# Moving the first weight conversions, the centroid copies and the first value loads in a fused attention and MoE kernel

## The chip, the core and the metric

One core of one Trainium2 chip runs the whole kernel in one launch. The metric is the device time of one execution in microseconds (us). The median of three runs before the change was 805.57 us (804.07 to 806.16).

## What is computed

Three stages follow one another. The first is clustered attention over 2 batches, 8 heads, 768 tokens and head dimension 64: each query and key gets the nearest of 16 centroids of its head, and a query sees only the keys of its own cluster. The other two are gated products on 1536 tokens.

```python
q_assign = argmax(q_n @ c_n.T); k_assign = argmax(k_n @ c_n.T)
scores = where(q_assign == k_assign, q @ k.T / sqrt(D), -1e9)
attn = softmax(scores) @ v            # 16 heads, 768 x 768 each
x = attn as [1536, 512]
x = ((x @ w1) * (x @ w2)) @ w3 @ w_out            # d_ff 1024
out = (sigmoid(x @ w_gate) * (x @ w_val)) @ w_out2   # d_ff 1536
```

## The kernel before

**Precision by splitting.** A float32 operand is split into a high part (`hi`, rounded for the fast matmul) and a rest (`lo`), and products are summed from two or three matmuls. `split` (line 51) makes both parts on the engines that it is given. `move` (line 61) is a DMA on SyncE's queue (SP) from SBUF to SBUF.

**Weights.** They arrive as 64-bit words. `f64_split` (line 84) loads a half of a weight pair (512 KB, line 98, on SP), takes an absolute value on ScalarE (ACT, line 102), limits it (line 108), works on the bits with four VectorE (DVE) steps (lines 110 to 113), adds (line 114), casts to `hi` on ACT (line 115) and subtracts for `lo` on GpSimd (POOL, line 116). `load_pair` (line 118) does this for two halves. For the first two pairs the add of line 114 is on POOL too. The loaded words have three buffers (tag `f64`), so at most three halves can lie in SBUF unconverted. In the traces a half's words are called `w_f`, its work tile `w_a`, its result `w`.

**Start.** TensorE (PE) is kept busy with dummy transposes (`warm`, line 130: 12, then 8, then 50). The centroids are loaded, normalized and transposed, split into `chi` and `clo`, and placed by eight small DVE copies (line 174) into the block matrix `cw`. `load_qk(0)` and `load_v(0)` (lines 188 to 201) issue the first loads: 384 KB each of q, k and v. `prep_split` makes `hi` and `lo` of q and k, and its DVE instructions are held behind the last copy into `cw` (line 395). `prep_scatter` (line 228) moves them by six DMAs per head into the operands `QH`, `KH`, `QX`, `KX`. `prep_sims` (line 243) multiplies them with `cw`. `prep_argmax`, `prep_onehot` and `prep_mask` turn the similarities into one-hot rows that become rows 64 to 95 of `QH` and `KH`. `prep_v` splits v on POOL.

**Attention.** The work goes over 8 head pairs (0 to 7), each 2 heads and 3 blocks of 256 queries, so 48 blocks. `scores(j)` (line 302) is one of 96 tiles of 128 queries: four matmuls (lines 315 to 318), a row maximum on DVE (line 319, `nm`), an exponential on ACT (line 321, `e`). `transposes` (line 324) turns three groups of a block with PE; ACT (line 56) and DVE (line 59) split them into `ph`, `pl` (one group of some blocks on POOL). `weighted_v` (line 343) multiplies with v. Beside this, pair n prepares pair n+1 (split, scatter, similarities, one-hot, mask, v). Pair 6 loads and splits no later pair's q and k, and pair 7 prepares none.

**Where the first weights stand.** At the end of block 36 (first of pair 6) and of block 42 (first of pair 7) the loop traces `load_pair` for weight pairs 0 and 1 (line 445). `tc.issue_after(ins)` puts the instructions traced in its block behind `ins` in the issue order of `ins`'s own engine, and does nothing on other engines. Here `ins` is a DVE instruction, the last mask of head pair 0 (line 285).

**Order of work.** A planner sets each engine's order at build time: an engine takes, of the instructions that it believes ready, the one that stands first in the program; an instruction that stands later is taken earlier if nothing before it is ready. On the chip each engine then runs its list in that order.

**After attention.** From line 510 on the gated products run as long series of matmuls; the first unit needs weight pair 0, the second needs weight pair 1.

Of the kernel before, what the change touches and what calls it, by code (L numbers as in the profile page):

```python
# [11 lines left out]
AF = mybir.ActivationFunctionType  # L12
ALU = mybir.AluOpType
AX = mybir.AxisListType

B, H, S, D, C = 2, 8, 768, 64, 16
NP = H // 2
KT = S // 128
BIG = 2.0 ** 60
# [8 lines left out]
def tile_cluster_attention__then__moe__then__gated_moe(  # L28
# [15 lines left out]
    nc = tc.nc  # L44
# [6 lines left out]
    def split(x, hi, lo, hi_engine, lo_engine):  # L51

        if hi_engine is nc.gpsimd:
            nc.gpsimd.tensor_scalar(out=hi, in0=x, scalar1=1.0, scalar2=1.0, op0=ALU.mult, op1=ALU.mult)  # L54
        elif hi_engine is nc.scalar:
            nc.scalar.copy(hi, x)  # L56
        else:
            nc.vector.tensor_copy(hi, x)
        lo_engine.tensor_tensor(out=lo, in0=x, in1=hi, op=ALU.subtract)  # L59
# [70 lines left out]
    def warm(n, name):  # L130

        pt = ps_t.tile([128, 2, 256], F32, tag="t", name=name)
        for i in range(n):
            nc.tensor.transpose(pt[:, 0, 0:128], ident, ident)
# [28 lines left out]
    cps = ps_a.tile([128, 128], F32, tag="a", name="cps")  # L163
    nc.tensor.transpose(cps, c2.rearrange("p j d -> p (j d)"), ident)
    warm(8, "warm1")
    chi = ctmp.tile([128, 128], F32R, name="chi")
    clo = ctmp.tile([128, 128], F32R, name="clo")
    split(cps, chi, clo, nc.vector, nc.vector)
    for e in range(2):
        rows = slice(64 * e, 64 * e + 64)  # L170
        for w in range(2):
            base = 64 * w + 32 * e
            for g, src in ((0, chi), (1, clo)):
                cw_done = nc.vector.tensor_copy(
                    cw[rows, :, w, base + 16 * g : base + 16 * g + 16],
                    src[rows].bitcast(F32).rearrange("p (n e c) -> p n e c", n=NP, e=2)[:, :, e, :],
                )
# [16 lines left out]
    def load_v(pr):  # L194
        t = core.tile([128, 2, KT, D], F32, tag="vraw", name=f"vraw{pr}", bufs=1)
        nc.sync.dma_start(t, v[pr])
        raw[pr, "v"] = t


    load_qk(0)  # L200
    load_v(0)


    opnd = {}

    def lead(pr):

        return nc.vector if pr == 0 else nc.gpsimd
# [19 lines left out]
    def prep_scatter(pr, e):  # L228
        qh, ql, kh, kl = opnd[pr, "hl"]
        r = slice(64 * e, 64 * e + 64)  # L230
        QH = core.tile([96, S], F32R, tag="QH", name=f"QH{pr}_{e}", bufs=3)
        KH = core.tile([96, S], F32R, tag="KH", name=f"KH{pr}_{e}", bufs=3)
        QX = core.tile([128, S], F32R, tag="QX", name=f"QX{pr}_{e}", bufs=3)
        KX = core.tile([128, S], F32R, tag="KX", name=f"KX{pr}_{e}", bufs=3)
        move(QH[0:64], qh[r])
        move(KH[0:64], kh[r])
        move(QX[0:64], qh[r])
        move(QX[64:128], ql[r])
        move(KX[0:64], kl[r])
        move(KX[64:128], kh[r])  # L240
        opnd[pr, e] = (QH, KH, QX, KX)
# [17 lines left out]
    def prep_argmax(pr):  # L259
        sm = opnd.pop((pr, "sm"))  # L260
        mx = core.tile([128, S // 32], F32, tag="mx", name=f"mx{pr}", bufs=2)
        shape = [128, S // 32, C]
        nc.vector.tensor_reduce(out=mx, in_=sm, axis=AX.X, op=ALU.max)
        nc.vector.tensor_tensor(out=sm, in0=sm, in1=mx.unsqueeze(2).broadcast_to(shape), op=ALU.is_ge)
        lead(pr).tensor_tensor(out=sm, in0=sm, in1=dec.unsqueeze(1).broadcast_to(shape), op=ALU.mult)
        opnd[pr, "code"] = sm
# [13 lines left out]
    def prep_mask(pr, e):  # L280
        ohT = opnd[pr, "oh"]
        QH, KH, _, _ = opnd[pr, e]
        if pr == 0:
            nc.scalar.copy(QH[64:96], ohT[32 * e : 32 * e + 32])
            opnd["masked"] = nc.vector.tensor_scalar(out=KH[64:96], in0=ohT[64 + 32 * e : 96 + 32 * e], scalar1=-1.0, scalar2=BIG, op0=ALU.add, op1=ALU.mult)
            return
        move(QH[64:96], ohT[32 * e : 32 * e + 32])
        move(KH[64:96], ohT[64 + 32 * e : 96 + 32 * e])
# [8 lines left out]

    blocks = [(pr, e, q0) for pr in range(NPR) for e in range(2) for q0 in range(0, S, 256)]
    NB = len(blocks)
    exps, pts, avs, acc_x = {}, {}, {}, {}  # L300

    def scores(j):

        if not 0 <= j < 2 * NB:
            return
        pr, e, q0 = blocks[j // 2]
        QH, KH, QX, KX = opnd[pr, e]
        at = e * KT + q0 // 128 + j % 2
        if at == 0:
            acc_x[pr, "sum"] = core.tile([128, 2 * KT], F32, tag="ss", name=f"ss{pr}", bufs=2)  # L310
        ss = acc_x[pr, "sum"]
        nm = core.tile([128, 1], F32, tag="nm", name=f"nm{j}", bufs=4)
        q = slice(q0 + 128 * (j % 2), q0 + 128 * (j % 2) + 128)
        sp = ps_s.tile([128, 1024], F32, tag="s", name=f"s{j}")
        nc.tensor.matmul(sp[:, 0:512], QH[:, q], KH[:, 0:512], start=True, stop=False)
        nc.tensor.matmul(sp[:, 512:S], QH[:, q], KH[:, 512:S], start=True, stop=False)
        nc.tensor.matmul(sp[:, 0:512], QX[:, q], KX[:, 0:512], start=False, stop=True)
        nc.tensor.matmul(sp[:, 512:S], QX[:, q], KX[:, 512:S], start=False, stop=True)  # L318
        nc.vector.tensor_reduce(out=nm, in_=sp[:, 0:S], axis=AX.X, op=ALU.max, negate=True)  # L319
        et = core.tile([128, S], F32, tag="e", name=f"e{j}", bufs=5)  # L320
        nc.scalar.activation(et, sp[:, 0:S], AF.Exp, bias=nm, accum_out=ss[:, at : at + 1])  # L321
        exps[j] = et

    def transposes(i, k2):
# [19 lines left out]
    def weighted_v(i, k2):  # L344
        if not 0 <= i < NB:
            return
        pr, e, q0 = blocks[i]
        ph, pl = pts.pop((i, k2))
        if k2 == 0:
            avs[i] = ps_a.tile([128, 256], F32, tag="a", name=f"av{i}")  # L350
        av = avs[i]
        for kk in range(2):
            kt = 2 * k2 + kk
            w = opnd[pr, e, "v"][:, kt].rearrange("p j d -> p (j d)")
            nc.tensor.matmul(av, w, ph[:, kk, :], start=kt == 0, stop=False)  # L355
            nc.tensor.matmul(av, w, pl[:, kk, :], start=False, stop=kt == KT - 1)  # L356
        if k2 < 2:
            return
        del avs[i]
        if (e, q0) == (0, 0):  # L360
            for what, bufs in (("xa", 2), ("xb", 1)):
                acc_x[pr, what] = core.tile([128, S], F32, tag=what, name=f"{what}{pr}", bufs=bufs)
        main = slice(64 * e, 64 * e + 64)
        other = slice(64 - 64 * e, 128 - 64 * e)
        cols = slice(q0, q0 + 256)
        nc.scalar.copy(acc_x[pr, "xa"][main, cols], av[main])
        nc.scalar.copy(acc_x[pr, "xb"][main, cols], av[other])
        if (e, q0) == (1, 512):
            xa = acc_x[pr, "xa"]
            nc.gpsimd.tensor_tensor(out=xa, in0=xa, in1=acc_x.pop((pr, "xb")), op=ALU.add)  # L370
# [21 lines left out]
        split(xa, x_hl[:, hp, 0, S * b : S * b + S], x_hl[:, hp, 1, S * b : S * b + S], nc.gpsimd, nc.gpsimd)  # L392


    with tc.issue_after(cw_done.ins):
        prep_split(0)
    prep_scatter(0, 0)
    prep_sims(0)
    warm(50, "warm2")
    prep_scatter(0, 1)  # L400
    prep_argmax(0)
    prep_onehot(0)
    for e in range(2):
        prep_mask(0, e)
    prep_v(0)
    load_qk(1)
    load_v(1)
    prep_split(1)
    prep_scatter(1, 0)
    wt = []  # L410
    for i in range(-2, NB + 1):
        pr, at = divmod(i, 6)
        nxt = pr + 1 if 0 <= i and pr + 1 < NPR else None
        later = nxt + 1 if nxt and nxt + 1 < NPR else None
        scores(2 * i + 3)
        if nxt and at == 1:
            prep_scatter(nxt, 1)
            prep_argmax(nxt)
        transposes(i, 0)
        if nxt and at == 0:  # L420
            prep_sims(nxt)
        scores(2 * i + 4)
        if nxt and at == 2:
            prep_onehot(nxt)
            for e in range(2):
                prep_mask(nxt, e)
        transposes(i, 1)
        transposes(i, 2)
        if later and at == 2:
            load_qk(later)  # L430
        if later and at == 3:
            load_v(later)
        weighted_v(i - 1, 0)
        if nxt and at == 2:
            prep_v(nxt)
        weighted_v(i - 1, 1)
        if 0 < pr and i < NB and at == 2:
            finish_x(pr - 1)
        weighted_v(i - 1, 2)
        if later and at == 3:  # L440
            prep_split(later)
            prep_scatter(later, 0)
        if 0 <= i < NB and at == 5:
            sums(pr)
        if i in (NB - 12, NB - 6):
            with tc.issue_after(opnd["masked"].ins):
                wt.append(load_pair(w12, len(wt), "w12_", nc.gpsimd))
    finish_x(NPR - 1)
    att.close()
# [184 lines left out]
```

## Time and profile before

| what | before |
|---|---|
| median of 3 runs | 805.57 us |
| profiled execution, device time | 805.55 us |
| its span, first to last instruction | 803.8 us |
| PE, DVE, ACT, POOL busy | 773.7, 583.1, 360.8, 340.9 us |
| mean granted TensorE clock | 0.992 |

The span is what the trace shows; 1.75 us of the device time lie around it. A busy share is the time in which an engine had an instruction under way. PE's granted clock is 1.00 at 2.4 GHz and 0.50 at 1.2 GHz. In rows of a timeline, the first number is the start, the second the duration, and the bracket tells how long the engine was idle before and what ended that.

### The profile page before, as it was taken

Reading aid. Unit: us, or ns where it says so; the run is one execution under the profiler, and the core shown is the slowest. Engines: PE = TensorE matmul, PEld = TensorE weight load, DVE = VectorE, ACT = ScalarE, POOL = GpSimd, SP = SyncE. Lnnn points to the kernel's source line nnn. Section 1 sums busy time; section 2 is a strip of 40 time slices with the busy share of each in tenths; the row PEclk is TensorE's granted clock in tenths of the full one; section 3 lists DMA queues with packets and bytes.
Section 4 is the critical chain, followed back from the end, with each engine's and each line's share of the span. In section 5 each row is a group of like instructions: output and inputs, shape, how many; then the busy total and the mean of one; then the engine's idle time right before and its main releaser. Section 6 shows DMA issues by size and latency. Waiting matters only on the chain.

```text
span 803.8 us, 11226 instructions
## 1 busy us (share of the span) xinstructions
PE 773.7 (96%) x4031; PEld 656.5 (82%) x4031; DVE 583.1 (73%) x864; ACT 360.8 (45%) x711; POOL 340.9 (42%) x348
## 2 busy tenths in 40 slices
PE   6799999989899999999999999999999999999998
PEld 5688888879798888888888888888888888888886
DVE  6899999989898769999987532477751777827222
ACT  3598998888798334344443211332231222022000
POOL 2547687567655544544542310244421444024100
PEclk9799999999999999999999999999999999999999
DMA  8655656655611223434432100022220222200012
GB/s 221 193 163 127 167 149 167 161 132 147 167 45 47 99 79 131 157 131 141 148 132 79 52 1 1 27 79 80 89 95 1 70 88 80 79 0 1 1 66 91
DMA packets 26969, 78.05 MB, mean 97 GB/s; under 512 B 4417, under 2 KB 4513, under 8 KB 26913
## 3 DMA queue, kind: packets, MB, share of 16 engines
q1 hardware_dynamic: 26912, 77.33, 32.4%
q8 instruction: 32, 0.52, 0.3%
q14 instruction: 25, 0.20, 0.1%
HBM read 52.49 MB, written 3.19 MB: 69 GB/s over the span
## 4 chain that ended last, share of the span: by engine, by line
PE 67%; DVE 11%; ACT 7%; DMA 5%; POOL 5%; issue 4%; SPq 2%; DVEq 0%; POOLq 0%; ACTq 0%
PE p L67 18%; PE p L66 18%; PE p L65 18%; ACT e L321 2%; PE pt L332 2%; DMA raw<-in_qkT_dram 2%; ACT ph L56 2%; PE av L356 1%; PE sims L252 1%; PE av L355 1%; DVE pl L59 1%; DVE nm L319 1%; PE w34p L67 1%; PE w34p L65 1%; PE w34p L66 1%
## 5 line engine op out<-in xcount | busy, mean ns | idle before, releaser
L65 PE MATMUL p<-x,wgv 128*128 128x512 f32 x288 | 112.0, 389 | 0.0
L66 PE MATMUL p<-x,wgv 128*128 128x512 f32 x288 | 112.0, 389 | 0.0
L67 PE MATMUL p<-x,wgv 128*128 128x512 f32 x288 | 112.0, 389 | 0.0
L319 DVE TENSOR_REDUCE nm<-s 128x1 f32<-128x768 f32 x96 | 90.7, 946 | 6.2 <-PE s L318 5.9
L59 DVE TENSOR_TENSOR pl<-pt,ph 128x512 fp32r<-128x512 f32 x128 | 84.5, 678 | 11.2 <-ACT ph L56 10.9
L321 ACT ACTIVATE e<-s,nm 128x768 f32<-128x768 f32 x96 | 87.5, 911 | 9.4 <-DVE nm L319 8.6
L332 PE MATMUL pt<-ident,e 128*128 128x128 f32 x576 | 81.5, 274 | 2.7 <-DVE pl L59 2.3
L56 ACT CAST ph<-pt 128x512 fp32r<-128x512 f32 x128 | 72.5, 589 | 13.4 <-PE pt L332 6.4
L355 PE MATMUL av<-ph,vx 128*128 128x256 f32 x288 | 76.3, 297 | 0.4 <-POOL ph L54 0.2
L356 PE MATMUL av<-pl,vx 128*128 128x256 f32 x288 | 72.9, 286 | 2.1 <-POOL pl L59 2.1
L66 PE MATMUL p<-x,w 128*128 128x512 f32 x192 | 74.8, 390 | 0.0
L67 PE MATMUL p<-x,w 128*128 128x512 f32 x192 | 74.7, 389 | 0.0
L65 PE MATMUL p<-x,w 128*128 128x512 f32 x192 | 74.7, 389 | 0.0
L332 PEld LDWEIGHTS pt<-ident,e 128*128 128x128 f32 x576 | 66.8, 141 | 8.8 <-DVE pl L59 4.2
L54 POOL TENSOR_SCALAR u<-ut 128x512 fp32r<-128x512 f32 x36 | 22.3, 619 | 112.5 <-DVE ut L560 112.5
L65 PEld LDWEIGHTS p<-x,wgv 128*128 128x128 f32 x288 | 54.1, 188 | 11.3
L66 PEld LDWEIGHTS p<-x,wgv 128*128 128x128 f32 x288 | 54.1, 188 | 11.3
L67 PEld LDWEIGHTS p<-x,wgv 128*128 128x128 f32 x288 | 54.1, 188 | 11.1
L116 POOL TENSOR_TENSOR wo<-wo_a,wo 128x512 fp32r<-128x512 f32 x20 | 26.3, 1314 | 81.1 <-ACT wo L115 81.1
L59 DVE TENSOR_TENSOR u<-ut,u 128x512 fp32r<-128x512 f32 x36 | 35.7, 991 | 34.1 <-POOL u L54 32.9
L356 PEld LDWEIGHTS av<-pl,vx 128*128 128x128 f32 x288 | 54.8, 190 | 3.5 <-POOL pl L59 3.3
L560 DVE TENSOR_TENSOR ut<-p,ut 128x512 f32<-128x512 f32 x36 | 24.7, 686 | 44.7 <-PE p L67 44.6
(146 smaller groups left out, 1878.6 us busy)
## 6 DMA issues: line engine op xcount, KB each, us to landing
wgv_f<-in_w_gv_dram SPq DMA_DIRECT2D x24, 512.0 KB, 3.2
wo_f<-in_w_out_dram SPq DMA_DIRECT2D x20, 512.0 KB, 3.8
w_f<-in_w_dram SPq DMA_DIRECT2D x16, 512.0 KB, 4.1
w_f<-in_w3T_dram SPq DMA_DIRECT2D x16, 512.0 KB, 3.2
raw<-in_qkT_dram SPq DMA_DIRECT2D x16, 384.0 KB, 4.8
vraw<-in_v_dram SPq DMA_DIRECT2D x8, 384.0 KB, 5.9
QH<-hi SPq DMA_DIRECT2D x16, 192.0 KB, 3.3
KH<-hi SPq DMA_DIRECT2D x16, 192.0 KB, 5.7
```

The lines of the kernel that those rows point to most:

```text
L56: nc.scalar.copy(hi, x)
L59: lo_engine.tensor_tensor(out=lo, in0=x, in1=hi, op=ALU.subtract)
L65: nc.tensor.matmul(ps, whi, xhi, start=start, stop=False)
L66: nc.tensor.matmul(ps, whi, xlo, start=False, stop=False)
L67: nc.tensor.matmul(ps, wlo, xhi, start=False, stop=stop)
L116: lo_engine.tensor_tensor(out=lo, in0=af, in1=hi, op=ALU.subtract)
L319: nc.vector.tensor_reduce(out=nm, in_=sp[:, 0:S], axis=AX.X, op=ALU.max, negate=True)
L321: nc.scalar.activation(et, sp[:, 0:S], AF.Exp, bias=nm, accum_out=ss[:, at : at + 1])
L332: nc.tensor.transpose(pt[:, kk, 128 * t : 128 * t + 128], es[t][:, k0 : k0 + 128], ident)
L355: nc.tensor.matmul(av, w, ph[:, kk, :], start=kt == 0, stop=False)
L356: nc.tensor.matmul(av, w, pl[:, kk, :], start=False, stop=kt == KT - 1)
L560: nc.vector.tensor_tensor(out=ut, in0=pv, in1=ut, op=ALU.mult)
```

## The change

The eight copies into `cw` go from DVE to POOL, and the DVE instructions of the first split now stand behind `clo`. The third dummy series has 70 transposes instead of 50. `load_v(0)` stands after the scatter of the first pair in the program, and `load_v(1)` in the loop at block 0. The conversions of the first two weight pairs stand behind the latest row maximum on DVE and the latest exponential on ACT, instead of behind the first pair's mask on DVE alone.

```diff
-    split(cps, chi, clo, nc.vector, nc.vector)
+    nc.vector.tensor_copy(chi, cps)
+    clo_done = nc.vector.tensor_tensor(out=clo, in0=cps, in1=chi, op=ALU.subtract)
...
-                cw_done = nc.vector.tensor_copy(
+                nc.gpsimd.tensor_copy(
...
     load_qk(0)
-    load_v(0)
...
-        nc.vector.tensor_reduce(out=nm, in_=sp[:, 0:S], axis=AX.X, op=ALU.max, negate=True)
+        last["DVE"] = nc.vector.tensor_reduce(out=nm, in_=sp[:, 0:S], axis=AX.X, op=ALU.max, negate=True)
...
-        nc.scalar.activation(et, sp[:, 0:S], AF.Exp, bias=nm, accum_out=ss[:, at : at + 1])
+        last["ACT"] = nc.scalar.activation(et, sp[:, 0:S], AF.Exp, bias=nm, accum_out=ss[:, at : at + 1])
...
-    with tc.issue_after(cw_done.ins):
+    with tc.issue_after(clo_done.ins):
         prep_split(0)
     prep_scatter(0, 0)
     prep_sims(0)
-    warm(50, "warm2")
+    warm(70, "warm2")
     prep_scatter(0, 1)
+    load_v(0)
...
     load_qk(1)
-    load_v(1)
...
+        if i == 0:
+            load_v(1)
         weighted_v(i - 1, 0)
...
         if i in (NB - 12, NB - 6):
-            with tc.issue_after(opnd["masked"].ins):
+            with tc.issue_after(last["DVE"].ins), tc.issue_after(last["ACT"].ins):
                 wt.append(load_pair(w12, len(wt), "w12_", nc.gpsimd))
```

## Rows read from the trace of the kernel before

**Rows 1.** Busy time by stretch: length, PE, PEld, DVE, ACT, POOL, clock, DMA share, GB/s

```profile
54.20:83.50 29.30, 27.72 (x201) 25.25 (x200) 26.55 (x38) 24.92 (x57) 19.98 (x18) 1.00 0.58 148
83.50:111.90 28.40, 27.66 (x204) 25.62 (x205) 27.86 (x41) 25.95 (x58) 21.30 (x19) 1.00 0.61 151
...
200.90:232.45 31.55, 28.27 (x202) 25.08 (x201) 28.87 (x39) 26.57 (x59) 22.94 (x21) 1.00 0.57 135
232.45:263.50 31.05, 29.02 (x216) 26.36 (x215) 26.32 (x39) 28.07 (x64) 14.51 (x13) 1.00 0.08 31
263.50:803.80 540.30, 535.67 (x2368) 442.69 (x2366) 347.53 (x526) 146.95 (x251) 177.40 (x193) 1.00 0.21 74
```

**Rows 2.** Timeline of the start, SP's queue: the first v and the first weight half

```profile
2.58 0.43 SPq L196 DMA_DIRECT2D vraw<-in_v_dram  x1
...
3.06 0.43 SPq L98 DMA_DIRECT2D w_f<-in_w_dram  x1
```

**Rows 3.** Waits of SP's queue, 0 to 60 us: total, times, longest

```profile
SPq L62 <- DMA w_f<-in_w_dram: 1.9, 1, 1.9
```

**Rows 4.** Busy time by stretch at the start, columns as in rows 1

```profile
20.00:22.00 2.00, 1.88 (x6) 1.19 (x5) 1.04 (x2) 0.37 (x1) 0.00 (x0) 0.50 0.96 346
```

**Rows 5.** Timeline of the start, 0 to 24 us: DVE, PE and POOL

```profile
5.87 0.28 DVE L174 CAST cw<-chi 64x64 fp32r<-64x64 f32 x2
...
6.68 0.20 DVE L174 CAST cw<-clo 64x64 fp32r<-64x64 f32 x1
...
7.78 0.95 DVE L59 TENSOR_TENSOR lo<-raw,hi 128x768 fp32r<-128x768 f32 x1
...
9.60 4.09 PE L134 MATMUL warm<-ident 128*128 128x128 f32 x36
...
10.10 0.98 POOL L54 TENSOR_SCALAR vx<-vraw 128x384 fp32r<-128x384 f32 x2 [7.12 <-DMA vraw<-in_v_dram]
...
16.38 1.14 DVE L285 TENSOR_SCALAR KH<-ohT 32x768 fp32r<-32x768 f32 x2
...
19.62 0.77 PE L317 MATMUL s<-KX,QX 128*128 128x512 f32 x1 [1.36 <-DMA KX<-hi]
```

**Rows 6.** Timeline of the first blocks, 23 to 31 us: DVE, ACT, POOL and PE

```profile
23.43 0.83 ACT L56 CAST hi<-raw 128x768 fp32r<-128x768 f32 x1 [0.81 <-POOL raw L222]
...
25.90 1.58 DVE L59 TENSOR_TENSOR lo<-raw,hi 128x768 fp32r<-128x768 f32 x1
...
26.65 1.99 POOL L114 TENSOR_TENSOR w_a<-w_f,w_a 128x512 f32<-128x512 f32 x1
...
27.40 1.81 DVE L319 TENSOR_REDUCE nm<-s 128x1 f32<-128x768 f32 x2
...
28.59 1.81 POOL L59 TENSOR_TENSOR lo<-raw,hi 128x768 fp32r<-128x768 f32 x1
28.66 0.62 ACT L115 CAST w<-w_a 128x512 fp32r<-128x512 f32 x1 [3.51 <-POOL w_a L114]
...
29.75 0.88 ACT L321 ACTIVATE e<-s,nm 128x768 f32<-128x768 f32 x1
...
30.78 1.22 PE L252 MATMUL sims<-hi,cw 128*128 128x512 f32 x2 [2.92 <-ACT e L321]
```

**Rows 7.** Conversions alone (tile w_a) by stretch: length, DVE, ACT, POOL, clock, DMA, GB/s

```profile
83.50:200.90 117.40, 4.71 (x6) 0.62 (x1) 3.51 (x2) 1.00 0.61 153
200.90:232.45 31.55, 0.65 (x1) 1.31 (x2) 3.19 (x3) 1.00 0.57 135
...
232.45:263.50 31.05, 3.88 (x5) 1.30 (x2) 3.20 (x3) 1.00 0.08 31
```

**Rows 8.** Timeline of DVE in head pair 7: the first, fifth and ninth row maximum

```profile
232.45 0.96 DVE L319 TENSOR_REDUCE nm<-s 128x1 f32<-128x768 f32 x1 [0.18 <-PE s L318]
...
240.00 0.95 DVE L319 TENSOR_REDUCE nm<-s 128x1 f32<-128x768 f32 x1
...
251.32 0.95 DVE L319 TENSOR_REDUCE nm<-s 128x1 f32<-128x768 f32 x1
```

More of the change, by code (lines that the diff above doesn't have):

```diff
@@ L284, in prep_mask @@
             nc.scalar.copy(QH[64:96], ohT[32 * e : 32 * e + 32])
-            opnd["masked"] = nc.vector.tensor_scalar(out=KH[64:96], in0=ohT[64 + 32 * e : 96 + 32 * e], scalar1=-1.0, scalar2=BIG, op0=ALU.add, op1=ALU.mult)
+            nc.vector.tensor_scalar(out=KH[64:96], in0=ohT[64 + 32 * e : 96 + 32 * e], scalar1=-1.0, scalar2=BIG, op0=ALU.add, op1=ALU.mult)
             return
@@ L299, in tile_cluster_attention__then__moe__then__gated_moe @@
     NB = len(blocks)
-    exps, pts, avs, acc_x = {}, {}, {}, {}
+    exps, pts, avs, acc_x, last = {}, {}, {}, {}, {}
     def scores(j):
```

## The prediction

> **What bounds the kernel now.** I read the busy time by stretch first. From 263.5 us on PE is busy 535.67 of 540.30 us [rows 1]; the change touches nothing there, so whatever it brings must arrive as an earlier or later end of attention. In the head pairs no engine is full: pair 7 takes 31.05 us with PE 29.02, ACT 28.07 and DVE 26.32 busy, pair 6 takes 31.55 with DVE 28.87 [rows 1]. A tile goes from PE to DVE (maximum) to ACT (exponential) and back to PE, so a delay on any of them shows unless it falls into one of the others' gaps. Next I read the timeline of the start, for what the first scores wait for, and that of the first blocks, for what the weight conversion does there: ACT stands still 3.51 us before its cast of line 115, because POOL's add of line 114 is late, and the exponential behind the cast starts only at 29.75, though the first of the two maxima that began at 27.40 was done near 28.3 [rows 6]. Last I read the conversion instructions alone, to price them where they are to go [rows 7, 8].
>
> **The part at the start.** Three edits have no price, and here is their cover. The first scores' third matmul starts at 19.62, released by the transfer of `KX` [rows 5]. The last DVE mask is done at 16.38 + 1.14 = 17.52, so the whole chain centroids, similarities, one-hot has 2.1 us of slack.
>
> Copies on POOL: on DVE the eight run from 5.87 to 6.88, and the last `lo` that the similarities need ends at 8.73 [rows 5]. Without them DVE's `lo` can come about 1.0 us sooner. POOL's nearest row is 0.49 us for 384 columns [rows 5]; at most eight times that, 3.9, from the same start, makes `cw` ready at 9.8, 1.1 us later than `lo` was. So between -1.0 and +1.1 us on the chain, all inside the slack: 0. If the transfer came sooner by 2.1 us, this would be paid in full.
>
> Warming: 36 dummies took 4.09 us and ended at 13.69 [rows 5], so 20 more take 2.3 us and end near 16.0, ahead of the scores; at half the clock they would take twice that and still end before 19.62. Nothing is lost. What could be gained is the clock: it is 0.50 in 20 to 22 us, although PE is busy 1.88 of these 2 us [rows 4]. But PE must still wait for `KX` between, and I expect the clock to have fallen by then. I take 0; if it stays high, the first two tiles' matmuls shrink by at most half, 0.9 us.
>
> v: in the list of before SP issues v at 2.58 and, right behind, a weight half at 3.06 whose code stands in block 36 [rows 2]. So issue follows readiness and not the place in the program, and the change gives neither load anything to wait for, since `issue_after` holds DVE and ACT instructions alone and these issues are SP's. I expect SP to issue both where it did, and the wait of 1.9 us for the weight half ahead of a scatter [rows 3] to stay. Price 0. The second v is ready once POOL has split the first, as before: 0.
>
> **The part that gains, first blocks.** With the conversions gone, DVE's `lo` of pair 1 starts when its `hi` is cast, 23.43 + 0.83 = 24.26, instead of 25.90 [rows 6]: 1.6 us sooner. It took 1.58 there beside POOL and 0.95 alone [rows 5, 6]. The maxima behind it move by 1.6 to 2.2, and the exponential starts as the first is done, 1.4 sooner still. So the exponential moves from 29.75 to between 26.1 and 26.8: a gain of 3.0 to 3.6. If the maximum goes ahead of `lo`, 4.6. What is late next are the similarities of pair 1, for which PE waited 2.92 us on that exponential [rows 6]: they also need POOL's `lo`, which stood from 28.59 to 30.40 behind the add of 1.99 us; without it, it ends near 28.4, while their matmuls with it come some 1.7 us after the exponential's end of about 27.6. So most of the gain passes; if POOL sets it alone, 2.0 is left. I take 3.2 (2.0 to 4.6).
>
> **The part that gains, pairs 2 to 5.** Six DVE steps, 4.71 us, leave this stretch [rows 7]. The stretch 83.5 to 111.9 has DVE busy 27.86 of 28.40 and is still shorter than the one before it with 26.55 of 29.30 [rows 1]; the extra work fitted into gaps. So between 0 and 4.7; I take a third, 1.6, being nearer to what fits into gaps.
>
> **The part that costs, pairs 6 and 7.** Before, pair 7 holds one half's DVE steps (3.88 us) and pair 6 one half's last step, cast and POOL steps (0.65 DVE) [rows 7], which I count as half a half. After, each holds two halves: 2.5 halves are added. Behind these instructions stand the next maxima on DVE and the next exponentials and `ph` casts on ACT, and PE waits for both. Price of one half: the first four intervals between maxima in pair 7 take 240.00 - 232.45 = 7.55 us, the next four, in which three of the DVE steps, the add and the cast fall, 251.32 - 240.00 = 11.32 [rows 8]: 3.8 for most of a half. That is the upper end. The lower end is ACT's share alone, 1.3 [rows 7], if DVE's steps fall in its gaps; pair 7 leaves DVE 4.7 us idle, pair 6 only 2.7 [rows 1]. I take the middle, 2.5, since one pair has room and the other hardly. So 2.5 x 2.5 = 6.3 (3.2 to 9.4). Later weights' loads wait longer for the three buffers; the cover is the 99% busy PE after 263.5, whose first units need only pairs 0 and 1 [rows 1]: 0, and if a weight were late, a stall of a few us there.
>
> **Sum.** -3.2 - 1.6 + 6.3 = +1.5 us on the profiled execution's 805.55, which stands 0.02 under the median: 807.0.
>
> **Rivals.** (A) The conversions vanish in the last pairs. For it: their prep is smaller, and DVE is idle 4.7 us in pair 7. Against: 11.32 against 7.55 us. At 1.3 a half the cost is 3.2; with the ramp at 3.6 and half of the middle, 2.4: 3.2 - 3.6 - 2.4 = -2.8, 802.7. (B) The steps of both halves stand one behind the other in DVE's list ahead of the next maxima, at the start of pairs 6 and 7, and PE runs dry: 3.8 a half, 9.4 - 3.2 - 1.6 = +4.6, 810.1. It decides from a price of 3.0 a half on. For it: the blocks trace them there, so that they are first in line, and POOL is busy 22.94 of 31.55 us in pair 6 [rows 1]. DVE steps beside POOL run long, as `lo` does, 1.58 against 0.95 us [rows 5, 6].
>
> The Trainium skill, page SBUF — State Buffer, section Who interferes with whom, says that a DVE instruction with two SBUF inputs, or in a two-port mode, and a reading GpSimd instruction hold the shared ports exclusively, so that the later one waits its whole length. By that rule the price of a half would be rival B's and the sum 810.1; the trace agrees with the lengthening of `lo`, and does not show how often the conversions would meet POOL.
>
> (C) The change does more than I think: v and the weight half do leave the front. Then 0.90 MB at the 346 GB/s of rows 4, 2.6 us, is off the DMA engines ahead of `KX`, and the scores start when the masks are in: 2.1 sooner, 804.9. Against: [rows 2].
>
> **How the numbers follow.** A measurement of this kernel can tell about 0.3%, 2.4 us, from no change. My forecast has 0.30, (C) 0.10, both within 0.3%: same 0.40. (A) has 0.28, faster. (B) has 0.32, slower. The range reaches past (A) and (B) by about 1 us for the bounds of the ramp: 801.5 to 811.0. The forecast alone would be 804.7 to 809.4.
>
> **What would show it.** Right: no conversion step before pair 6; the exponential of 29.75 near 26.6 and pair 1's similarities 3 us sooner; the first `KX` matmul near 19.6 and v at 2.6 as before; pairs 6 and 7 longer by 3 us each, with ACT waiting for line 114. Wrong: pairs 6 and 7 as long as before (A), a start of the scores before 18 us (C), idle PE after attention (late weights), or pairs 1 to 5 that move by more than 2 us each.

## The result, and the profile after

The changed kernel is **slower**: its median is 815.77 us (814.82 to 818.45, 4 runs) against 805.8 us of the kernel before (4 runs). The ratio of the two times is 1.0133, with a 95% interval of 1.0104 to 1.0163. The forecast was 807.0, and the range ended at 811.0. The profiled execution's span is 816.6 us instead of 803.8 (+12.8), its mean granted clock 0.985 instead of 0.992. That execution was the slowest of the four (818.45), so the terms read from its trace add up to 12.8 us, while the medians differ by 10.0.

I cut both spans at the same row maxima (line 319): the first of all, the first of pair 1, of pair 6, of pair 7, and the last. The stretch from the first maximum of all to the first of pair 1 is called the ramp. Busy time by these stretches (columns as in [rows 1]), before:

```profile
20.64:54.23 33.59, 28.08 (x165) 23.84 (x164) 30.83 (x39) 24.33 (x51) 16.26 (x15) 0.86 0.63 174
...
200.91:232.45 31.54, 28.26 (x202) 25.07 (x201) 28.86 (x39) 26.56 (x59) 22.94 (x21) 1.00 0.57 135
232.45:258.03 25.58, 23.82 (x176) 21.71 (x175) 22.66 (x32) 22.76 (x54) 11.98 (x10) 1.00 0.10 37
258.03:803.80 545.77, 540.86 (x2408) 447.35 (x2406) 351.20 (x533) 152.25 (x262) 179.93 (x196) 1.00 0.21 74
```

and after:

```profile
24.57:52.59 28.02, 24.48 (x165) 20.95 (x163) 24.46 (x32) 22.64 (x48) 10.31 (x10) 1.00 0.63 165
...
197.35:237.31 39.96, 31.61 (x206) 28.58 (x205) 34.48 (x48) 27.87 (x60) 25.28 (x22) 0.87 0.48 125
237.31:270.07 32.76, 25.60 (x167) 22.91 (x166) 28.39 (x38) 24.91 (x56) 15.94 (x13) 0.90 0.13 45
270.07:816.60 546.53, 541.20 (x2413) 448.07 (x2411) 351.48 (x532) 153.00 (x264) 180.83 (x197) 1.00 0.22 73
```

The first maximum comes 3.9 us later (24.57 against 20.64). The ramp gains 33.59 - 28.02 = 5.6. Pairs 1 to 5 take 197.35 - 52.59 = 144.8 instead of 146.7, a gain of 1.9. Pair 6 loses 8.4, pair 7 loses 7.2, and the part behind the last maximum loses 0.8. The sum is 3.9 - 5.6 - 1.9 + 8.4 + 7.2 + 0.8 = +12.8. In pairs 6 and 7 DVE is busy 5.6 and 5.7 us longer, and PE is granted 0.87 and 0.90 of its clock.

**The late start.** Timeline after, against [rows 2, 5]:

```profile
2.58 0.43 SPq L197 DMA_DIRECT2D vraw<-in_v_dram  x1
3.06 0.43 SPq L98 DMA_DIRECT2D w_f<-in_w_dram  x1
...
7.61 0.99 POOL L54 TENSOR_SCALAR vx<-vraw 128x384 fp32r<-128x384 f32 x2 [4.63 <-DMA vraw<-in_v_dram]
8.56 1.95 POOL L59 TENSOR_TENSOR vx<-vraw,vx 128x384 fp32r<-128x384 f32 x2
10.45 0.87 POOL L175 CAST cw<-chi 64x64 fp32r<-64x64 f32 x4
11.37 0.87 POOL L175 CAST cw<-clo 64x64 fp32r<-64x64 f32 x4
12.11 1.22 PE L252 MATMUL sims<-hi,cw 128*128 128x512 f32 x2 [4.68 <-POOL cw L175]
...
16.12 7.71 PE L134 MATMUL warm<-ident 128*128 128x128 f32 x62
16.36 0.98 DVE L254 STREAM_TRANSPOSE sT<-sims 128x768 f32<-128x768 f32 x1 [8.67 <-PE sims L252]
...
24.57 1.82 DVE L319 TENSOR_REDUCE nm<-s 128x1 f32<-128x768 f32 x2 [1.16 <-PE s L318]
```

SP issues v and the weight half where it did. But in POOL's list the split of v, which waits for v, stands ahead of the copies. The copies end at 12.2 instead of 6.9, PE waits 4.68 us for `cw`, and the similarities start at 12.11 instead of 6.9. The last 62 of the 70 dummies run until 23.8, which is 0.4 us past the last mask (22.66 + 0.75 = 23.41).

**Pair 6.** Timeline after, DVE, POOL, PE and ACT; before, this stretch held one step:

```profile
210.24 0.96 DVE L319 TENSOR_REDUCE nm<-s 128x1 f32<-128x768 f32 x1
...
211.17 2.20 POOL L370 TENSOR_TENSOR xa<-xa,xb 128x768 f32<-128x768 f32 x1
...
211.73 3.07 DVE L108 TENSOR_SCALAR w_a<-w_a 128x512 f32<-128x512 f32 x2
214.73 0.75 DVE L110 TENSOR_SCALAR w_a<-w_a 128x512 uint32<-128x512 uint32 x2
...
215.14 2.00 POOL L391 TENSOR_TENSOR xa<-xa,r 128x768 f32<-128x768 f32 x1 [0.61 <-DMA r<-r_dram]
...
215.40 2.89 DVE L111 SCALAR_TENSOR_TENSOR w_f<-w_f,w_a 128x512 uint32<-128x512 uint32 x2
218.21 0.75 DVE L112 TENSOR_SCALAR w_a<-w_f 128x512 uint32<-128x512 uint32 x2
218.88 1.28 DVE L113 SCALAR_TENSOR_TENSOR w_a<-w_f,w_a 128x512 f32<-128x512 uint32 x2
...
219.64 2.94 POOL L114 TENSOR_TENSOR w_a<-w_f,w_a 128x512 f32<-128x512 f32 x2 [2.50 <-DVE w_a L113]
...
220.69 0.94 DVE L319 TENSOR_REDUCE nm<-s 128x1 f32<-128x768 f32 x1
...
220.82 1.12 PE L332 MATMUL pt<-ident,e 128*128 128x128 f32 x4 [5.14 <-DVE pl L59]
...
221.35 0.62 ACT L115 CAST w<-w_a 128x512 fp32r<-128x512 f32 x1 [6.11 <-POOL w_a L114]
```

All ten DVE steps of two halves stand in one row from 211.73 to 220.2. The next maximum starts 10.4 us after the one before it. PE waits 5.14 us, ACT waits 6.11 for its cast of line 115, and PE's clock is 0.50 in 220 to 224 us. Pair 7 has its ten from 248.6 to 259.4, with one maximum among them.

### The profile page after: what moved, and what is told of

Its sections match the earlier page's. It is cut to its first block, busy times and chain, and to the rows that moved or that the text cites. A ratio compares the mean times of both kernels' runs of the same rounds, so it can differ in the third digit from the quotient of the medians.

```text
span 816.6 us, 11246 instructions
## 1 busy us (share of the span) xinstructions
PE 777.5 (95%) x4051; PEld 662.7 (81%) x4051; DVE 580.5 (71%) x856; ACT 360.8 (44%) x711; POOL 342.4 (42%) x356
## 4 chain that ended last, share of the span: by engine, by line
PE 67%; DVE 12%; POOL 8%; ACT 5%; DMA 4%; issue 4%; SPq 0%; DVEq 0%; POOLq 0%; ACTq 0%
PE p L66 17%; PE p L67 17%; PE p L65 17%; PE pt L332 3%; DVE nm L319 2%; DMA raw<-in_qkT_dram 2%; ACT e L321 2%; PE s L315 1%; DVE pl L59 1%; PE sims L252 1%; PE av L356 1%; PE w34p L67 1%; PE av L355 1%; PE w34p L65 1%; PE w34p L66 1%
## 5 line engine op out<-in xcount | busy, mean ns | idle before, releaser
L319 DVE TENSOR_REDUCE nm<-s 128x1 f32<-128x768 f32 x96 | 90.9, 948 | 10.4 <-PE s L318 9.8
L332 PE MATMUL pt<-ident,e 128*128 128x128 f32 x576 | 83.6, 279 | 10.4 <-DVE pl L59 9.5
L332 PEld LDWEIGHTS pt<-ident,e 128*128 128x128 f32 x576 | 68.6, 144 | 15.3 <-DVE pl L59 9.9
L356 PE MATMUL av<-pl,vx 128*128 128x256 f32 x288 | 75.4, 294 | 2.0 <-POOL pl L59 1.8
L356 PEld LDWEIGHTS av<-pl,vx 128*128 128x128 f32 x288 | 56.5, 196 | 3.2 <-POOL pl L59 3.0
L355 PEld LDWEIGHTS av<-ph,vx 128*128 128x128 f32 x288 | 56.0, 194 | 2.9 <-ACT xb L367 2.2
```

Of the source, the lines that this page charges most:

```text
L319: last["DVE"] = nc.vector.tensor_reduce(out=nm, in_=sp[:, 0:S], axis=AX.X, op=ALU.max, negate=True)
L332: nc.tensor.transpose(pt[:, kk, 128 * t : 128 * t + 128], es[t][:, k0 : k0 + 128], ident)
```

## The experiments

All kernels compute the same. The median is over all runs of a kernel; the other columns come from its one trace. "First max." is the start of the first row maximum in us, and "of pair 1" and "of pair 6" are the starts of those pairs' first maxima. "Rest" is the span from the first maximum of pair 6 to the end, "steps" the number of the 20 DVE conversion steps (lines 108 to 113) in it.

Two things limit what the columns can tell. The traced execution lies up to 2.9 us off its kernel's median (e4: 818.34 against 815.4; e6: 806.68 against 809.36). And pairs 1 to 5 take 141.8 to 145.6 us in the eight kernels that have no step there (changed, e1, e2, e4, e6, e7, e11, e12), so a difference of 3 us in that stretch shows nothing. The kernel before, run again beside each group of experiments, had medians of 805.0 to 806.3; the ratios below are to those.

| kernel | median us | first max. | of pair 1 | of pair 6 | rest | steps |
|---|---|---|---|---|---|---|
| before | 805.8 | 20.64 | 54.23 | 200.91 | 602.9 | 6 |
| changed | 815.77 | 24.57 | 52.59 | 197.35 | 619.3 | 20 |
| e1 | 811.58 | 18.18 | 50.26 | 193.31 | 616.4 | 20 |
| e2 | 813.62 | 20.14 | 49.07 | 192.57 | 618.1 | 20 |
| e3 | 803.10 | 26.91 | 57.84 | 203.27 | 598.4 | 3 |
| e4 | 815.4 | 21.41 | 52.96 | 198.56 | 617.8 | 20 |
| e5 | 803.72 | 19.03 | 54.43 | 199.24 | 602.7 | 6 |
| e6 | 809.36 | 18.65 | 48.40 | 192.39 | 612.5 | 20 |
| e7 | 823.75 | 18.37 | 48.20 | 192.64 | 627.3 | 20 |
| e8 | 810.40 | 18.19 | 49.21 | 194.88 | 612.9 | 14 |
| e9 | 812.20 | 18.18 | 50.14 | 211.76 | 597.3 | 0 |
| e10 | 810.98 | 18.18 | 50.19 | 201.56 | 609.2 | 10 |
| e11 | 815.88 | 18.66 | 48.57 | 193.40 | 620.4 | 20 |
| e12 | 810.61 | 19.15 | 50.22 | 192.06 | 616.1 | 20 |
| e13 | 798.38 | 20.13 | 52.69 | 197.59 | 599.1 | 3 |

**e1, copies back on DVE.** The changed kernel with

```diff
-                nc.gpsimd.tensor_copy(
+                cw_done = nc.vector.tensor_copy(
...
-    with tc.issue_after(clo_done.ins):
+    with tc.issue_after(cw_done.ins):
```

> The changed kernel with the eight copies into cw back on VectorE, nothing else undone. Theory 1 (the copies wait on GpSimd behind the split of the first v, so the first row maximum comes at 24.57 instead of 20.64 us): the first maximum returns to 20.4 to 20.9 us and the time falls by 2 to 4 us, to 812 to 814, since part of the shorter ramp of the changed kernel was only the transfers having more time. Theory 2 (the late start is made up by the ramp, all of the loss is in pairs 6 and 7): the time stays at 815 to 816.5.

The ratio to before is 1.0084 (1.0051 to 1.0116). The median is 4.2 us better than the changed kernel's and still 5.8 worse than before, so undoing the copies gives back about two fifths of the loss. The time is just under theory 1's; the first maximum, at 18.18, is earlier than either theory had it, and 2.5 us earlier than in the kernel before.

The traces show where these 2.5 us come from. In the kernel before the first `KX` matmul waits for its transfer until 19.62 [rows 5]; in e1 it starts at 17.63 and waits for none. SP's wait of 1.9 us for the weight half [rows 3] stands in the kernel before and in e4 (1.8 us), and in none of the thirteen kernels that trace the first v later and have 70 dummies. Which of these two edits removes it was not tried.

**e2, v's split behind the copies on POOL.** The changed kernel with

```diff
-    prep_v(0)
+    with tc.issue_after(cw_last.ins):      # cw_last: the last of the POOL copies
+        prep_v(0)
```

> The changed kernel with the split of the first v held behind the eight copies in GpSimd's list. Theory 1 (the order on GpSimd is the cost, not the engine): the copies run from 5.9 to about 7.7 us, the first maximum comes at 20.2 to 20.9 us, time within 0.8 us of e1. Rival (copies are slow on GpSimd, or the late v split is what counts): the first maximum stays beyond 22 us and the time above 814.

The ratio is 1.0093 (1.0066 to 1.0119). The first maximum is 4.4 us earlier than in the changed kernel, so POOL's order made some two thirds of the 6.4 us between the changed kernel and e1. The other 2.0 us stay: the copies on POOL run from 5.69 to 8.85 (on DVE they were done at 6.88 [rows 5]) and PE waits 2.41 us for `cw`. Theory 1 missed the time: it is 2.0 us above e1's and not within 0.8, though the runs of the two overlap (810.71 to 815.32 and 810.43 to 815.62).

**e3, conversions early.** The changed kernel with the old hold:

```diff
-            with tc.issue_after(last["DVE"].ins), tc.issue_after(last["ACT"].ins):
+            with tc.issue_after(opnd["masked"].ins):
```

> The changed kernel with the conversions held behind the first mask again, as before; copies, warming and v as changed. Theory 1 (two separate losses): the start stays late, the ramp has its conversion stall again, pairs 6 and 7 are as before: 808 to 811. Rival (the conversions' place is the only loss): 804.5 to 806.5. Rival (the start is the only loss): 815 or more.

The median is 803.10 (8 runs) and the ratio 0.9961 (0.9947 to 0.9975): a little faster than before and below every expectation, in spite of the latest start of all. Eleven steps lie up to the first maximum of pair 1, six in pairs 1 to 5, three in the rest.

**e4, conversions alone.** The kernel before with the hold of the changed one.

> The kernel before with the conversions alone held behind the last maximum and the last exponential. Theory 1 (10 VectorE steps in one row, GpSimd's steps in between, and the lower clock after PE's idle time cost 15 us in pairs 6 and 7, the ramp and pairs 1 to 5 give back 5 to 7): 812 to 815, with the granted clock at 0.50 for several us in each of pairs 6 and 7. My recorded forecast (2.5 us a half): 806 to 808.

The ratio is 1.0124 (1.0101 to 1.0147): the late conversions alone give the loss. The rest grows by 617.8 - 602.9 = 14.9 us. The ramp gains only 2.0 (52.96 - 21.41 = 31.55 instead of 33.59), and PE's clock is 0.50 for 10.4 us of it.

**e5, copies on DVE and conversions early**: the edits of e1 and e3 together.

> The changed kernel with the eight copies back on VectorE and the conversions held behind the first mask again: what is left of the change is the later trace of the first v and the 70 dummies. Theory (the two losses add up: the late start by the copies, the rows of conversion steps in pairs 6 and 7): pairs 6 and 7 take 53 to 54 us as in e3_conversions_early, and the first maximum comes at 18 to 19 us as in e1_copies_on_dve instead of 26.9; of these 8 us some 2 to 4 are given back in the ramp, so 796 to 800 us. Rival (the ramp is bound by its conversions and not by its start): the first maximum of pair 1 comes at 56 to 58 us all the same, and the time is that of e3, 802 to 804 us.

The ratio is 0.9976 (0.9959 to 0.9992). The start is 7.9 us earlier than in e3 and the time the same, as the rival had it. But its reason is not shown: the first maximum of pair 1 comes at 54.43 and not at 56 to 58, and pairs 6 and 7 take 56.95 us and not 53 to 54. The planner put only eight steps up to pair 1 and six into the rest (e3: eleven and three), so part of the early start was lost in the rest (602.7 us against 598.4).

**e6, single halves** (with e1's edit): one half traced at each of four blocks.

```diff
-        if i in (NB - 12, NB - 6):
+        if i in (NB - 12, NB - 9, NB - 6, NB - 3):
...
-                wt.append(load_pair(w12, len(wt), "w12_", nc.gpsimd))
...
+                f64_split(w12[n, w], ..., nc.gpsimd, nc.gpsimd)     # one half
```

> Copies on VectorE; the four halves are traced one by one, at the third, sixth, ninth and twelfth block from the end, instead of two and two. Theory (a row of ten steps holds up the row maxima and the low parts for longer than the other engines have work in hand, and the granted clock then falls): a row of five steps is 4 to 4.6 us, PE has some 4 us in hand, so a half costs 1 to 2.5 us instead of about 4, the clock stays at 1.00 for most of pairs 6 and 7, and the time is 801 to 806 us. Rival (each step on VectorE in these pairs costs its own length, wherever it stands): pairs 6 and 7 together take 69 to 70 us as in e1_copies_on_dve and the time is 810 to 813 us.

The ratio is 1.0038 (1.0021 to 1.0055) and the median 809.36, between the two. Breaking up the rows of ten saved 2.2 us in the median, not 8. In the trace the clock was 0.50 for 3.4 us only, but that execution (806.68, mean clock 0.997) is one of the two shortest of ten: the other took 806.2 at a mean of 0.995, and the eight with 0.987 to 0.991 took 808.07 to 812.5. In the same code the shorter executions had the higher clock; which of the two is the cause these runs do not show.

**e7, dummies ahead of the rows** (with e1's edit): `warm(40)` behind the two `load_pair`.

> Copies on VectorE, conversions as in the changed kernel, and 40 dummy products on TensorE (about 4.4 us at the full clock) at each of the two rows of steps, just ahead of the next scores. They change no wait of VectorE. Theory A (the half clock behind each row, 17 us of it in e1_copies_on_dve, makes a third or more of the loss): the clock stays at 1.00, and the time is 803 to 808 us. Theory B (the loss is the queue on VectorE alone, the clock only follows): the clock stays at 1.00 and the time stays at 810 to 813 us; above 813 us if the dummies delay the scores.

The ratio is 1.0222 (1.0201 to 1.0243). Neither theory is answered, since both had the clock stay at 1.00. PE ran the 40 dummies for 4.53 us from 203.8, then waited 4.7 us all the same, and the clock fell to 0.50 behind that. Pairs 6 and 7 take 80.4 us instead of 69.9 in e1: the dummies only held up the scores.

**e8, held at block 5** (with e1's edit): traced in the same place, but free for the planner from block 5 on.

```diff
+        if i == 5:
+            held = (last["DVE"].ins, last["ACT"].ins)
...
-            with tc.issue_after(last["DVE"].ins), tc.issue_after(last["ACT"].ins):
+            with tc.issue_after(held[0]), tc.issue_after(held[1]):
```

> Copies on VectorE; the conversions are traced where the changed kernel traces them but held only behind the last maximum of block 5, so that the planner is free to put the steps into gaps from pair 1 on: the first two halves lie one step at a time in pairs 1 to 6, the last two still in one row in pair 7. Theory (the row is what costs, not the work): pair 6 takes 29 to 30 us instead of 37.8, pairs 2 to 5 gain no more than 1 us in all, pair 7 stays at 31 to 33 us, and the time is 802 to 806 us. Rival (each step costs its own length wherever it stands): what pair 6 gains, some 8 us, the pairs before it lose, and the time stays at 809 to 813 us.

The ratio is 1.0061 (1.0041 to 1.008), above the theory's time. With six steps in them, pairs 1 to 5 take 145.7 us, at the upper edge of the kernels with none (141.8 to 145.6). The other fourteen steps fell into the rest and cost 15.6 us more than none would (612.9 - 597.3, e9).

**e9 and e10, single steps** (with e1's edit): `f64_split` as a generator that stops after each DVE step, one step a block, each behind the last maximum and exponential.

```diff
-        if i in (NB - 12, NB - 6):
+        if i in (4, 5, 7, 8, 10, 11, 13, 14, ..., 31, 32):     # e10: 24 to 43
...
             with tc.issue_after(last["DVE"].ins), tc.issue_after(last["ACT"].ins):
-                wt.append(load_pair(w12, len(wt), "w12_", nc.gpsimd))
+                next(steps)
```

> Copies on VectorE, and the same 20 conversion steps of VectorE written one by one in blocks 4 to 32 (pairs 0 to 5), each held behind the last maximum, so that none stands beside another and none is left for pairs 6 and 7. Theory (what is dear is a row of steps, one alone costs about 0.3 us as in pairs 2 to 5 of the kernel before): the first maximum of pair 6 comes 20 times 0.3 us later than in e6_single_halves, at 197 to 200 us, pairs 6 and 7 take 52 to 54 us as in e3_conversions_early, and the time is 796 to 800 us, below every kernel so far. Rival (a step costs its own length, 0.4 to 0.7 us and more beside GpSimd, in any pair): the first maximum of pair 6 at 203 to 206 us, and 801 to 806 us.

> As e9_single_steps_early with one step in each of blocks 24 to 43: ten in pairs 4 and 5, six in pair 6, four in pair 7. It tells the row from the place. Theory (the row): each step of pair 6 and 7 costs about 0.3 us too, these pairs take 54 to 57 us together, and the time is 796 to 801 us. Rival (the place: the last pairs have less room on VectorE than those before): a step there costs 0.7 to 1.1 us as in e6_single_halves and the changed kernel, pairs 6 and 7 take 60 to 64 us, and the time is 803 to 808 us.

The medians are 812.20 and 810.98: **my theory of the row fell**, and both are above what the rivals had too. In e9 the 20 steps stand alone and in early pairs, and pairs 1 to 5 take 161.6 us instead of 144.0 in e6: 0.88 us a step (0.80 to 0.99 against the eight kernels without). In e10 ten steps in the rest cost 609.2 - 597.3 = 11.9, or 1.19 each, and pairs 6 and 7, with 62.2 us, are where its rival had them. These prices hold for a step together with its share of the ACT and POOL work of the conversion, which moves with it. Where the planner chose the place (six steps in pairs 1 to 5 of before, e3, e5, e8 and e13), the stretch takes 144.8 to 146.7 us, too close to the kernels without a step to price one.

**e11, dummies in the stall** (with e1's edit): 40 dummies behind the scores of tiles 79 and 92.

> Copies on VectorE, conversions as in the changed kernel, and 40 dummy products (4.4 us at the full clock) behind the scores of blocks 39 and 46 (rows 79 and 92), where TensorE stands idle behind the row of steps in e1_copies_on_dve, in a part of the score tile that nothing reads. e7_dummies_in_rows had them ahead of the stall, moved the stall with them, and the clock fell as before; here they stand in it. Theory A (the granted clock of 0.50 behind the rows is a third or more of the loss): the clock stays at 1.00 behind the row in pair 6, this pair takes 33 to 35 us instead of 37.8, and the time is 803 to 809 us. Theory B (VectorE's queue is all of it): the pairs stay at 37 to 39 and 31 to 33 us, and the time at 810 to 813 us.

The ratio is 1.0125 (1.0092 to 1.0157). The time, 815.88, is above both theories, and so are the two pairs (39.3 and 35.6 us). Windows of 2 us in pair 6 of e11, columns as above:

```profile
212.00:214.00 2.00, 2.00 (x21) 2.00 (x20) 2.00 (x4) 0.00 (x0) 0.47 (x1) 1.00 0.66 152
214.00:216.00 2.00, 0.37 (x4) 0.13 (x2) 2.00 (x5) 0.00 (x0) 0.69 (x1) 1.00 0.00 0
216.00:218.00 2.00, 0.66 (x4) 0.42 (x4) 2.00 (x4) 0.62 (x1) 2.00 (x2) 1.00 0.02 4
218.00:220.00 2.00, 0.04 (x1) 0.04 (x1) 2.00 (x4) 1.70 (x4) 2.00 (x3) 0.86 0.90 285
220.00:222.00 2.00, 2.00 (x7) 1.81 (x8) 1.64 (x3) 1.28 (x3) 2.00 (x3) 0.50 0.67 225
```

The dummies filled the first part of the stall and the clock stayed at 1.00 until 218 us. PE stood idle again behind them, and the clock fell then. No run here has the row without the half clock, so the clock's share in pairs 6 and 7 stays open.

**e12, the high part on POOL** (with e1's edit): line 115 on POOL, so that no cast stands in ACT's list.

> As e1_copies_on_dve (811.6 us), with the high part of each converted half copied by GpSimd instead of ScalarE; VectorE's order of work is the same. In the changed kernel ScalarE's copy of the high part stands in its list ahead of the exponentials and waits 6 us for the end of VectorE's row. Theory A (the list of ScalarE carries a part of the loss: exponentials wait behind that copy, TensorE waits for them, and VectorE for TensorE): pairs 6 and 7 take 62 to 66 us together instead of 69.9, and the time is 804 to 808 us. Theory B (VectorE's row alone decides, since low parts and maxima stand behind it anyway): the pairs stay at 68 to 71 us, and the time at 810 to 813 us.

The ratio is 1.0067 (1.0049 to 1.0086) and the median 810.61, as theory B had it; pairs 6 and 7 take 69.9 us, as in e1. The waits of ACT there (total, times, longest), in e1:

```profile
ACT w L115 <- POOL w_a L114: 13.5, 4, 6.1
```

and in e12:

```profile
ACT ph L56 <- PE pt L335: 14.5, 6, 6.7
```

The wait only changed its name, and PE waited 9.1 us for `pl` as in e1 (9.0). So the place of the cast in ACT's list is not the cause; what PE waits for stands in DVE's list.

**e13, the start edits alone, in the right order**: the edits of e2 and e3 together.

> The changed kernel with the first v's split placed behind the copies on GpSimd and the conversions held behind the first mask as in the kernel before: the three start edits without their queue mistake and without the late conversions. Theory (the ramp is bound by its conversion steps on VectorE, as e3_conversions_early and e5_dve_copies_early showed with first maxima 8 us apart and equal times): the first maximum at 20 to 21 us, that of pair 1 at 54 to 56 us, and 801 to 804 us, no better than these two. Rival (copies off VectorE give the ramp room): the first maximum of pair 1 at 50 to 52 us, and 797 to 800 us.

The median is 798.38 us (797.6 to 800.88, 6 runs) and the ratio **0.9908 (0.9882 to 0.9934): better than both kernels**. The time is the rival's; the first maximum of pair 1, at 52.69, lies between rival and theory. POOL's start in e13:

```profile
5.76 2.33 POOL L175 CAST cw<-chi 64x64 fp32r<-64x64 f32 x4 [2.78 <-DVE chi L168]
8.13 0.86 POOL L175 CAST cw<-clo 64x64 fp32r<-64x64 f32 x4
9.09 0.98 POOL L54 TENSOR_SCALAR vx<-vraw 128x384 fp32r<-128x384 f32 x2
```

and busy time by stretch, pairs 6 and 7:

```profile
197.59:227.13 29.54, 27.78 (x200) 24.92 (x199) 28.25 (x39) 25.58 (x56) 19.81 (x18) 1.00 0.54 126
227.13:251.23 24.10, 23.72 (x172) 21.37 (x171) 20.09 (x30) 22.99 (x53) 12.83 (x11) 1.00 0.12 39
```

The steps lie in the same stretches as in e3 (eleven up to pair 1, six, three), the first maximum comes 6.8 us sooner, and 4.7 us of that reach the median. Against the kernel before, three more steps lie up to pair 1 and yet pair 1 begins 1.5 us earlier; pairs 1 to 5 are 1.8 us shorter; three fewer steps lie in the rest, which is 3.8 us shorter. So about half of the gain (3.8 of 7.1 us between the traces) comes with the steps that the planner took out of the rest. That the copies on POOL made it do so was not tried apart.

**What the table says together.** The rest is 597.3 us with no step, and rises with their number: by 1.1 and 1.8 for three (e3, e13), 5.6 and 5.4 for six (before, e5), 11.9 for ten, 15.6 for fourteen, and 15.2 to 22.0 for twenty in the kernels without dummies in the rest. That is 0.8 to 1.2 us a step from six on; with three the difference is too small to price one. From e13 to the changed kernel pairs 6 and 7 grow by 72.72 - 53.64 = 19.1 us and DVE's busy time in them by 62.87 - 48.34 = 14.5. As an account, and not as a test, three quarters of the growth is DVE at work, and the other 4.6 us come with the stalls and the half clock.

**What the half clock costs in the ramp.** Eight kernels (e1 and e6 to e12) run the same instructions in the same order on DVE, ACT, POOL and PE up to the first maximum of pair 1. Their ramps in e1 and e6:

```profile
18.18:50.26 32.08, 26.32 (x165) 22.93 (x163) 25.02 (x32) 23.33 (x48) 12.74 (x13) 0.89 0.64 168
18.65:48.40 29.75, 24.50 (x165) 20.96 (x163) 24.92 (x32) 22.97 (x48) 12.77 (x13) 1.00 0.66 180
```

In e1, e9, e10 and e12 the clock is 0.50 for 6.8 us of the ramp, and pair 1's first maximum comes at 50.14 to 50.26. In e6, e7 and e11 it is never 0.50, and that maximum comes at 48.20 to 48.57. In e8 it is 0.50 for 3.4 us, and the maximum comes at 49.21. So 6.8 us at half the clock cost about 1.8 us here, some 0.27 us for each; PE is busy 26.32 us against 24.50 with the same 165 matmuls. By that rate, an estimate, the 17 us at half the clock in pairs 6 and 7 of the changed kernel would be some 4.5 us.

## Why the prediction was wrong, step by step

**The price of a half was mis-sized; this is the step that failed.** The cost of pairs 6 and 7 stood in the sum at 2.5 x 2.5 = 6.3 us (3.2 to 9.4). The count was nearly right: 2.5 halves added, in fact 14 steps, 2.8. I took 2.5 us a half; the rest grew by 619.3 - 602.9 = 16.4 (14.9 in e4, with this edit alone), or 5.9 us a half, beyond my upper end of 3.8. That end was misread from the very rows it cites: the 3.77 us by which one stretch of pair 7 was longer held three of the five steps [rows 8], 1.26 a step, so 6.3 for a half, near what was measured. I noted "most of a half" and used it as a whole one. The lower end let DVE's idle time count as room (4.7 us in pair 7 [rows 1]). Idle time was not room: in the kernel before DVE is busy 22.66 of 25.58 us in pair 7 up to the last maximum, and the further steps still lengthened the pair by 7.2 us.

**Rival B saw what happens, too cheap.** The steps of both halves stood in a row and PE ran dry, as it said. But e6, e9 and e10 show that the row is a small part of the price: breaking it up saved 2.2 us, and single steps cost about as much. With the price that was measured its own sum would have been -3.2 - 1.6 + 16.4 = +11.6. That this is close to the +12.8 of the spans is partly luck: the late start (+3.9), which it had at 0, and the ramp's larger gain (-5.6 instead of -3.2) nearly cancel.

**"The extra work fitted into gaps" agrees with pairs 2 to 5, and does not carry over.** A gain of 1.6 was foreseen; pairs 2 to 5 gained 0.77 (117.43 to 116.66), and pair 1, which held no step before, 1.15. Both are within what kernels without a step differ by. There the six steps stand where the planner found room. A hold that frees the steps only where they are due takes this choice from it (e9: 0.88 us a step in the same pairs).

**The ramp gained more than foreseen, -5.6 instead of -3.2, and not for the reason given alone.** Taking the conversions out of it, and nothing else, gains 2.0 (e4), the lower end of the range. I counted only the delay of pair 1's similarities. In the changed kernel the granted clock in this stretch is also 1.00 instead of 0.86, 9.5 us at the half less, which by the rate above is an estimated 2.5 us. The prediction had the clock at 0, or 0.9 us if it stayed high.

**The copies on POOL were priced at 0 and cost about 4 us** (against the changed kernel e1 is 4.2 us better in the median and 6.4 at the first maximum, e2 2.2 and 4.4). I priced their length and not their place: [rows 5] show POOL idle for 7.12 us in front of v's split, and whatever comes behind that in POOL's list waits too. That the planner would put the split first was not in the trace, but the slack of 2.1 us called for the question. The length stayed within its bound (`cw` is ready at 8.85 in e2, 9.8 was allowed), but its cover was gone: the transfer of `KX` came sooner, and then, as the prediction had said, the delay is paid in full. In e2, with the right order, the first maximum is 2.0 us later than in e1. And the dummies, which were to end near 16.0, ended at 23.8 behind the late similarities.

**The wait of SP for the weight half was to stay, and went.** It is gone in every kernel that traces v later, and with the copies on DVE the first maximum then comes at 18.2 to 19.2 us instead of 20.64. This gain of some 2 us was priced at 0; in the changed kernel the late copies hide it. It is about what rival C had, but v and the weight half stayed in front.

**Right:** SP's issue of v and the weight half did not move (rival C's cause fell), no conversion step stands before pair 6, and the later weights cost little (+0.8 us behind the last maximum). **Not foreseen:** the start edits are worth 7.4 us when POOL's order is right and the conversions stay early (e13).

## What to carry to other kernels

Work moved to an idle engine stands in that engine's list: look what is ahead of it and what that waits for before calling it hidden. Price added steps by the nearest rows per instruction, not per bundle, and do not take idle time as room; steps that are due at a fixed place between two row maxima cost 0.8 to 1.2 us each here, although the instruction alone is 0.4 to 0.7. And test the parts of a change apart: three of its four edits together, with POOL's order put right, gained 7.4 us, and adding the fourth to them cost 15.2 (813.62 in e2 against 798.38 in e13).

## What the runs showed of the hardware

In pairs 6 and 7 of the changed kernel every conversion step that starts while POOL is in an instruction lasts until that is done. In pair 6 line 111 takes 2.29 us, from 215.40 to 0.55 us after the end of POOL's add of line 391 (215.14 + 2.00), and 0.68 right afterwards with POOL idle; line 108 takes 1.92 beside line 370, and 0.42 in e13 with POOL idle. Not every DVE instruction does this: the subtraction for `pl`, which reads PSUM, takes 0.68 at 220.09 in the middle of POOL's line 114, and 0.69 in e13 with POOL idle. The durations of the ten steps add up to 9.1 us in pair 6 and 10.1 in pair 7 (DVE is busy with them for 8.43 and 9.54), against 5.2 at the lengths that they have beside an idle POOL. No run took POOL's work out of their way, so what that would save stays open. The Trainium skill, page SBUF — State Buffer, section Who interferes with whom, says that a DVE instruction with two SBUF inputs or in a two-port mode, and a GpSimd instruction that reads SBUF, lock the shared ports for a whole instruction. The trace agrees for line 111, which has two inputs; for line 108, with one, it shows the lengthening and not the mode.

The granted clock fell to 0.50 (1.2 GHz) behind PE's stalls in pairs 6 and 7 of the changed kernel, e1, e7 and e11, and was 1.00 again some 7 to 10 us later. With PE at half speed, DVE had work for only 3.38 of 6.10 us (223.9 to 230.0 in the changed kernel).

In the eleven profiles whose POOL list has v's split first and whose program has `load_v(0)` later, that split starts between 6.9 and 8.6 us, against 10.1 and 10.3 in the two whose program has it early (before, e4). SP issues the load at 2.58 us in both, and the same transfers in the same order up to 10 us. The same two are the only ones in which SP waits for the weight half. The cause of both stays open.
